# Attention scores in half-row tiles of TensorE, two key chunks at a time, with unpadded keys and a reordered start

## The chip, the cores and the metric

One core of one Trainium2 chip. The metric is the device time of one execution in microseconds (us), taken over several executions on the same chip. A program on one core has no die to compare with, so a run counts as fast when it lies within 1.5% of the fastest of its kernel; all times here are of such runs. Engines: PE is TensorE, ACT is ScalarE, DVE is VectorE, POOL is GpSimd, SP issues transfers. PE's spans are modelled at their ends, so for PE I read starts, not durations.

## The reference

Eight batches of twelve heads, 448 positions, head size 64. Attention with normed queries and keys, then a feed-forward of 768 to 2048 to 768 without residual:

```python
q_n, k_n = (rmsnorm(q, g_q), rmsnorm(k, g_k))
scores = scale * np.matmul(q_n, k_n.transpose(0, 1, 3, 2))
...
attn = attn / (np.sum(attn, axis=-1, keepdims=True) + 1e-09)
return np.matmul(attn, v).astype(np.float32)
...
h = x @ w_in
g = h * (1.0 / (1.0 + np.exp(-1.702 * h)))
return (g @ w_out).astype(np.float32)
```

## The kernel before

Two heads form a head pair; there are 48. Positions are cut into four chunks of 112. The program order of every engine is made ahead of time: `_Order` plays a list of tasks with assumed durations, and emits each instruction when its turn comes there. An engine then runs its instructions strictly in that order. `od.add(name, engine, assumed ns, emit, priority, deps, lat, takes)`; `takes` names a buffer that must be free.

Keys lie zero padded: head 0 in rows 0 to 63 of one block of columns, head 1 in rows 64 to 127 of another, zeros elsewhere, so each score matmul uses all 128 rows of which 64 multiply zeros.

```python
def score(i, kc):                       # head pair i, key chunk kc
    sc = scs[i, kc] = ps_sc.tile([128, 2, 512], FP32, tag="sc", name="sc")   # 2 such buffers
    for hp in range(2):
        nc.tensor.matmul(sc[:SS, hp, :S],
                         lhsT=qk_ring[i % N_KZ][:, NS * (1 + hp) + kc, :],
                         rhs=qk_ring[i % N_KZ][:, :NS, :], start=True, stop=True)

def expo(i, kc):
    nc.scalar.activation(out=att_ring[i % N_ATT][:SS, kc, :, :S],
                         in_=scs.pop((i, kc))[:SS, :, :S], func=ACT.Exp)
...
od.add("gG", "DVE", 350, scale_g, -90, at=5000.0)        # product of the gains, early on DVE
...
od.add(("L", i, w), "SP", 400, ..., lat=moved(830.0))    # a load of 224 KB: 830 ns of the link
od.add(("S", i, j), "ACT", ..., i - 4.5, ...)            # squares for the norms, pair i
...
od.add(("C", i, kc), "PE", 380, lambda i=i, kc=kc: score(i, kc), i + kc / 4, ...,
       takes=("sc", ("E", i, kc)))
od.add(("E", i, kc), "ACT", 917, lambda i=i, kc=kc: expo(i, kc), i + kc / 4 - 1,
       deps=[("C", i, kc), ("P", i - N_ATT, 1, NS - 1)])
```

The value matmuls ("o" in the profile), the first feed-forward matmuls ("gp") and the second ("op") share PE with the scores ("sc"). The feed-forward of a batch can start only when its six head pairs are through attention, so PE has nothing but attention to do at first.

## Time and profile before

| | kernel before |
|---|---|
| time, median | 461.55 us (460.93 to 462.12, 4 runs) |
| span of the profiled execution | 460.4 us |
| first score matmul starts | 16.6 us |
| first feed-forward matmul starts | 55.0 us |
| last matmul ends | 455.6 us |

The two starts cut the run into a first part, in which PE waits for others, and a second, in which PE is the bound. The page's lines are shown in the prediction.

### The profile page before, as it was taken

Reading aid. Unit: us, or ns where it says so; the run is one execution under the profiler, and the core shown is the slowest. Engines: PE = TensorE matmul, PEld = TensorE weight load, DVE = VectorE, ACT = ScalarE, POOL = GpSimd, SP = SyncE. Lnnn points to the kernel's source line nnn. Section 1 sums busy time; section 2 is a strip of 40 time slices with the busy share of each in tenths; the row PEclk is TensorE's granted clock in tenths of the full one; section 3 lists DMA queues with packets and bytes.
Section 4 is the critical chain, followed back from the end, with each engine's and each line's share of the span. In section 5 each row is a group of like instructions: output and inputs, shape, how many; then the busy total and the mean of one; then the engine's idle time right before and its main releaser. Section 6 shows DMA issues by size and latency. Waiting matters only on the chain.

```text
span 460.4 us, 9576 instructions
## 1 busy us (share of the span) xinstructions
PE 435.3 (95%) x3728; PEld 271.9 (59%) x3728; DVE 219.0 (48%) x471; ACT 324.1 (70%) x463; POOL 196.5 (43%) x319
## 2 busy tenths in 40 slices
PE   0589999999999999999999999999999999999995
PEld 0356666666666665666666665666666665665563
DVE  3777888765653446515572347622551125403400
ACT  4587997888887778967886779866786677614421
POOL 4888986975272544434452635445343000000000
PEclk9997999999999999999999999999999999999998
DMA  8999999966868866587675885575323650021022
GB/s 204 266 243 255 250 244 231 214 185 158 163 136 155 234 160 152 130 186 166 155 168 119 216 192 131 124 172 144 66 57 74 105 121 16 17 78 36 0 70 69
DMA packets 111277, 67.48 MB, mean 147 GB/s; under 512 B 70272, under 2 KB 107648, under 8 KB 111232
## 3 DMA queue, kind: packets, MB, share of 16 engines
q1 hardware_dynamic: 105616, 60.35, 56.0%
q0 software_dynamic: 5376, 6.29, 7.8%
q8 instruction: 29, 0.48, 0.5%
q10 hardware_dynamic: 240, 0.23, 0.2%
q14 instruction: 16, 0.13, 0.1%
HBM read 45.61 MB, written 11.01 MB: 123 GB/s over the span
## 4 chain that ended last, share of the span: by engine, by line
PE 88%; POOL 3%; DVE 2%; DMA 2%; ACT 2%; issue 1%; SPq 1%; POOLq 0%; DVEq 0%; ACTq 0%
PE op L514 32%; PE gp L491 30%; PE sc L350 15%; PE o L362 10%; DMA gk<-in_g_k_dram 1%; POOL row L306 1%; ACT att L355 1%; PE t_ps L322 1%; DMA raw<-in_k_dram 1%; PE ot_ps L385 1%; DVE ssq L265 1%; DVE qk L332 0%; DVE obs L373 0%; POOL gq L174 0%; SPq L254 0%
## 5 line engine op out<-in xcount | busy, mean ns | idle before, releaser
L355 ACT ACTIVATE att<-sc 112x896 bf16<-112x896 f32 x192 | 173.9, 916 | 39.9 <-PE sc L350 37.9
L514 PE MATMUL op<-w_out_s,g 128*128 128x384 bf16 x896 | 167.5, 325 | 0.0
L491 PE MATMUL gp<-xt,w_in_s 128*128 128x448 bf16 x768 | 162.6, 352 | 0.0
L306 POOL TENSOR_TENSOR row<-raw,rs 112x512 bf16<-112x512 f32 x96 | 98.3, 1043 | 94.2 <-DMA qk<-row 84.6
L350 PE MATMUL sc<-qk 128*112 128x448 bf16 x384 | 109.4, 370 | 3.0 <-ACT att L355 1.4
L514 PEld LDWEIGHTS <-g 128*128 128x128 bf16 x896 | 81.1, 97 | 47.4 <-issue 0.3
L506 DVE SCALAR_TENSOR_TENSOR g<-th,gp 128x448 bf16<-128x448 f32 x128 | 78.0, 615 | 60.9 <-ACT th L500 60.8
L491 PEld LDWEIGHTS <-w_in_s 128*128 128x128 bf16 x768 | 71.0, 98 | 57.8
L362 PEld LDWEIGHTS <-att 112*128 112x128 bf16 x1536 | 82.2, 99 | 36.8 <-DVE obs L373 1.5
L500 ACT ACTIVATE th<-gp 128x448 f32<-128x448 f32 x128 | 69.3, 543 | 35.3 <-PE gp L491 35.1
L362 PE MATMUL o<-vx,att 112*128 112x65 bf16 x1536 | 90.8, 196 | 0.7 <-ACT att L355 0.4
L313 POOL TENSOR_TENSOR vx<-vraw,ones 112x512 bf16<-112x512 f32 x48 | 50.0, 1042 | 51.6 <-PE o L362 35.8
L265 DVE TENSOR_REDUCE ssq<-sq 112x16 f32<-112x1024 f32 (+1 forms) x50 | 58.4, 1174 | 27.9 <-ACT sq L259 27.7
L372 DVE RECIPROCAL rcp<-o 112x4 f32<-112x4 f32 x96 | 17.4, 181 | 112.0 <-PE o L362 111.4
L259 ACT ACTIVATE sq<-raw 112x1024 f32<-112x1024 f32 (+1 forms) x50 | 50.9, 1022 | 14.3 <-DMA raw<-in_k_dram 9.1
L524 ACT ACTIVATE osb<-op 128x384 f32<-128x384 f32 x56 | 27.3, 487 | 40.4 <-PE op L514 40.4
L350 PEld LDWEIGHTS <-qk 128*112 128x112 bf16 x384 | 44.0, 135 | 17.9 <-issue 4.0
L373 DVE TENSOR_TENSOR obs<-o,rcp 112x256 bf16<-112x256 f32 x96 | 40.7, 424 | 3.3
L343 ACT ACTIVATE qk<-qk,gG 128x448 bf16<-128x448 bf16 x36 | 23.9, 663 | 1.0 <-DMA qk<-row 0.9
L322 PE MATMUL t_ps<-ident,row 112*128 112x112 bf16 x96 | 9.6, 250 | 15.8 <-POOL row L306 15.7
L322 PEld LDWEIGHTS <-row 112*128 112x128 bf16 x96 | 7.2, 117 | 19.0 <-POOL row L306 17.5
L289 POOL TENSOR_TENSOR rs<-magic,seed 112x48 int32<-112x48 int32 (+1 forms) x16 | 4.5, 282 | 20.0 <-DVE seed L280 16.9
(37 smaller groups left out, 90.1 us busy)
## 6 DMA issues: line engine op xcount, KB each, us to landing
raw<-in_q_dram SPq DMA_DIRECT2D x48, 224.0 KB, 4.2
vraw<-in_v_dram SPq DMA_DIRECT2D x48, 224.0 KB, 3.9
raw<-in_k_dram SPq DMA_DIRECT2D x47, 224.0 KB, 4.7
w_in_s<-in_moe_w_in_dram POOLq DMA_DIRECT2D x4, 768.0 KB, 12.8
w_out_s<-in_moe_w_out_dram POOLq DMA_DIRECT2D x4, 768.0 KB, 11.3
out_dram<-osb SPq DMA_DIRECT2D x8, 336.0 KB, 3.3
out_dram<-osb SPq DMA_DIRECT2D x8, 288.0 KB, 2.7
out_dram<-osb SPq DMA_DIRECT2D x8, 240.0 KB, 2.9
```

The source lines that it names most:

```text
L259: nc.scalar.activation(out=sq_of[i][:SS, part], in_=raw[i][:SS, part], func=ACT.Square)
L265: nc.vector.reduce_sum(out=ssq_of[g0][:SS, i - g0, part], in_=sq_of[i][:SS, part], axis=AX.X)
L306: nc.gpsimd.tensor_tensor(out=row_view(i, gi)[:SS], in0=raw[i][:SS, gi], in1=y[:SS, a, gi].to_broadcast([SS, 2, NS, D]), op=ALU.mult)
L313: nc.gpsimd.tensor_tensor(out=vx[:, :, :D], in0=vr, in1=ones[:SS, :].to_broadcast([SS, 2 * NS, D]), op=ALU.mult)
L350: nc.tensor.matmul(sc[:SS, hp, :S], lhsT=qk_ring[i % N_KZ][:, NS * (1 + hp) + kc, :], rhs=qk_ring[i % N_KZ][:, :NS, :], start=True, stop=True)
L355: nc.scalar.activation(out=att_ring[i % N_ATT][:SS, kc, :, :S], in_=scs.pop((i, kc))[:SS, :, :S], func=ACT.Exp)
L362: nc.tensor.matmul(os_[i, hp][:, qs, :], lhsT=att_ring[i % N_ATT][:SS, kc, hp, qs * SS:qs * SS + WIN], rhs=vx_ring[i % N_V][:SS, hp, kc, : ...
L373: nc.vector.tensor_tensor(out=obs[i][:SS, :, hp, :], in0=o[:SS, :, :D], in1=rcp[:SS, :].to_broadcast([SS, NS, D]), op=ALU.mult)
L491: nc.tensor.matmul(ps[:, :], lhsT=w_in_s[:, ki, m * 128:(m + 1) * 128], rhs=xT[b][:, ki, :], start=(ki == 0), stop=(ki == KI - 1))
L500: nc.scalar.activation(out=th[:, :], in_=gps[b, m][:, :], func=ACT.Tanh, scale=0.851)
L506: nc.vector.scalar_tensor_tensor(out=g_of[b // 2][:, m, lo:lo + S], in0=ths.pop((b, m))[:, :], scalar=1.0, in1=gps.pop((b, m))[:, :], op0= ...
L514: nc.tensor.matmul(ops[bp, tm, hf][:, :], lhsT=g_of[bp][:, ko, tm * 128:(tm + 1) * 128], rhs=w_out_s[:, ko, hf * HALF:(hf + 1) * HALF], st ...
```

## The change

Its intent: let both heads' score matmuls run side by side in the two halves of PE's rows, and issue two key chunks together so that PE enters this mode half as often. Padding goes, so the transposing transfer from `row` to `qk` (the "crossbar" of the prediction) turns 8 blocks instead of 12, and DVE places keys with one instruction instead of two. The gains' loads move from POOL's queue to SP's, behind the first five loads, and their product on DVE moves behind the first pair's norms. The assumed durations of some tasks change too. A run of score matmuls with nothing else between them is called a group below; it has two matmuls before and four after.

```diff
-    def score(i, kc):
-        sc = scs[i, kc] = ps_sc.tile([128, 2, 512], FP32, tag="sc", name="sc")
-        for hp in range(2):
-            nc.tensor.matmul(sc[:SS, hp, :S],
-                             lhsT=qk_ring[i % N_KZ][:, NS * (1 + hp) + kc, :],
-                             rhs=qk_ring[i % N_KZ][:, :NS, :], start=True, stop=True)
+    def score(i, kcs):
+        for kc in kcs:
+            sc = scs[i, kc] = ps_sc.tile([128, 2, 512], FP32, tag="sc", name="sc")
+            for hp in range(2):
+                r = slice(64 * hp, 64 * hp + 64)
+                nc.tensor.matmul(sc[:SS, hp, :S], lhsT=qk_ring[i % N_KZ][r, 1, kc, :],
+                                 rhs=qk_ring[i % N_KZ][r, 0], start=True, stop=True)
 ...
-    od.add("gG", "DVE", 350, scale_g, -90, at=5000.0)
+    od.add("Lg", "SP", 1700, load_g, -5.2, lat=3000.0)
+    od.add("gG", "DVE", 350, scale_g, -0.5, deps=["Lg"])
 ...
-        for kc in range(NS):
-            od.add(("C", i, kc), "PE", 380, lambda i=i, kc=kc: score(i, kc), i + kc / 4,
-                   ... takes=("sc", ("E", i, kc)))
+        step = 1 if i < SINGLE else 2          # SINGLE = 2
+        for kc in range(0, NS, step):
+            kcs = range(kc, kc + step)
+            od.add(("C", i, kc), "PE", 190 * step + 130, lambda i=i, kcs=kcs: score(i, kcs),
+                   ... takes=("sc", [("E", i, c) for c in kcs]))
```

More of the change, by code (lines that the diff above doesn't have):

```diff
@@ L84, in run @@
                     if best.takes:
-                        self.slots[best.takes[0]][1].append(best.takes[1])
+                        self.slots[best.takes[0]][1].extend(best.takes[1])
                     best.emit()
@@ L119, in _fits @@
         n, held = self.slots[t.takes[0]]
-        if len(held) < n:
-            return True
-        back = self.named[held[-n]]
-        return back.end is not None and back.end <= now
+        for j in range(len(t.takes[1])):
+            if len(held) + j >= n:
+                back = self.named[held[j - n]]
+                if back.end is None or back.end > now:
+                    return False
+        return True
 @with_exitstack
@@ L153 @@
     ON_PE = NP * 2
+    SINGLE = 2
     ctx.enter_context(tc.manual_schedule())
@@ L170 @@
     gk = consts.tile([128, 1], FP32)
-    for t, src in ((gq, g_q), (gk, g_k)):
-        col = src.rearrange("(d o) -> d o", o=1)
-        for lo in (0, 64):
-            nc.gpsimd.dma_start(out=t[lo:lo + 64, :], in_=col)
     gG = consts.tile([128, 1], FP32)
@@ L180 @@
                 for j in range(N_ATT)]
-    qk_ring = [consts.tile([128, 3 * NS, SS], BF16, name=f"qk{j}", tag=f"qk{j}")
+    qk_ring = [consts.tile([128, 2, NS, SS], BF16, name=f"qk{j}", tag=f"qk{j}")
                for j in range(N_KZ)]
-    row_ring = [consts.tile([128, (3 * NS + 1) * 128], BF16, name=f"row{j}", tag=f"row{j}")
+    row_ring = [consts.tile([128, 2, NS, 128], BF16, name=f"row{j}", tag=f"row{j}")
                 for j in range(N_QKN)]
-    def row_view(j, gi):
-        t = row_ring[j % N_QKN]
-        if gi == 0 or j < ON_PE:
-            t = t[:, gi * NS * 128:(gi + 1) * NS * 128]
-            return t.rearrange("p (n h d) -> p h n d", h=2, d=D)
-        both = t[:, NS * 128:].rearrange("p (h r) -> p h r", h=2)[:, :, :NS * 128]
-        return both.rearrange("p h (n c) -> p h n c", c=128)[:, :, :, :D]
     vx_ring = [consts.tile([128, 2, NS, D + 1], BF16, name=f"vx{j}", tag=f"vx{j}")
                for j in range(N_V)]
-    for t in qk_ring:
-        nc.vector.memset(t[64:128, NS:2 * NS, :], 0.0)
-        nc.vector.memset(t[0:64, 2 * NS:, :], 0.0)
     for t in vx_ring:
@@ L301, in norm @@
         y, a = rs[i]
-        if gi == 1 and ON_PE <= i < ON_PE + N_QKN:
-            c = row_ring[i % N_QKN][:, NS * 128:3 * NS * 128].rearrange("p (n c) -> p n c", c=128)
-            nc.gpsimd.memset(c[:, :NS, D:], 0.0)
-            nc.gpsimd.memset(c[:, NS:, :D], 0.0)
         nc.gpsimd.tensor_tensor(
-            out=row_view(i, gi)[:SS], in0=raw[i][:SS, gi],
+            out=row_ring[i % N_QKN][:SS, gi].rearrange("p n (h d) -> p h n d", h=2), in0=raw[i][:SS, gi],
             in1=y[:SS, a, gi].to_broadcast([SS, 2, NS, D]), op=ALU.mult)
@@ L323, in turn_pe, with take_k @@
                     tps[i][:, gi, s, :],
-                    row_ring[i % N_QKN][:SS, (gi * NS + s) * 128:(gi * NS + s + 1) * 128],
-                    ident[:SS, :SS])
+                    row_ring[i % N_QKN][:SS, gi, s, :], ident[:SS, :SS])
     def take_q(i):
-        nc.vector.tensor_copy(out=qk_ring[i % N_KZ][:, :NS, :], in_=tps[i][:, 0])
-    def take_k(i, hp):
-        r = slice(64 * hp, 64 * hp + 64)
-        nc.vector.tensor_scalar(out=qk_ring[i % N_KZ][r, NS * (1 + hp):NS * (2 + hp), :],
-                                in0=tps[i][r, 1], scalar1=gG[r, :], scalar2=None,
-                                op0=ALU.mult)
+        nc.vector.tensor_copy(out=qk_ring[i % N_KZ][:, 0], in_=tps[i][:, 0])
+    def take_k(i):
+        nc.vector.tensor_scalar(out=qk_ring[i % N_KZ][:, 1], in0=tps[i][:, 1],
+                                scalar1=gG[:, :], scalar2=None, op0=ALU.mult)
     def turn_dma(i):
-        nc.sync.dma_start_transpose(out=qk_ring[i % N_KZ][:, :, :],
-                                    in_=row_ring[i % N_QKN][:SS, :3 * NS * 128])
+        nc.sync.dma_start_transpose(
+            out=qk_ring[i % N_KZ][:, :, :, :].rearrange("p g n s -> p (g n) s"),
+            in_=row_ring[i % N_QKN][:SS].rearrange("s g n c -> s (g n c)"))
     def scale_q(i):
-        t = qk_ring[i % N_KZ][:, :NS, :]
+        t = qk_ring[i % N_KZ][:, 0]
         nc.scalar.activation(out=t, in_=t, func=ACT.Identity, scale=gG[:, :])
     scs, os_ = {}, {}
-    def score(i, kc):
-        sc = scs[i, kc] = ps_sc.tile([128, 2, 512], FP32, tag="sc", name="sc")
-        for hp in range(2):
-            nc.tensor.matmul(sc[:SS, hp, :S],
-                             lhsT=qk_ring[i % N_KZ][:, NS * (1 + hp) + kc, :],
-                             rhs=qk_ring[i % N_KZ][:, :NS, :], start=True, stop=True)
+    def score(i, kcs):
[5 more added lines that the diff above has]
+                                 rhs=qk_ring[i % N_KZ][r, 0], start=True, stop=True)
     def expo(i, kc):
@@ L399, in scale_g, with load_g @@
                                 op0=ALU.mult)
-    od.add("gG", "DVE", 350, scale_g, -90, at=5000.0)
+    def load_g():
+        for t, src in ((gq, g_q), (gk, g_k)):
+            for lo in (0, 64):
+                nc.sync.dma_start(out=t[lo:lo + 64, :], in_=src.rearrange("(d o) -> d o", o=1))
+    od.add("Lg", "SP", 1700, load_g, -5.2, lat=3000.0)
+    od.add("gG", "DVE", 350, scale_g, -0.5, deps=["Lg"])
     for i in range(NG):
@@ L405 @@
         for w in range(3):
-            od.add(("L", i, w), "ACTQ" if i == 0 and w == 1 else "SP", 400,
+            od.add(("L", i, w), "ACTQ" if i == 0 and w == 1 else "SP", 480,
                    lambda i=i, w=w: load(i, w), i - 7 + (0, 0.1, 1.5)[w],
@@ L427 @@
                deps=[("L", i, 2), ("P", i - N_V, 1, NS - 1)])
-        kz_free = [("C", i - N_KZ, NS - 1)]
+        kz_free = [("C", i - N_KZ, NS - 1), ("C", i - N_KZ, NS // 2)]
         if i < ON_PE:
-            od.add(("T", i), "PE", 400, lambda i=i: turn_pe(i), i - 1.0,
-                   deps=[("N", i, 0), ("N", i, 1)], lat=250, takes=("w", ("K", i, 1)))
+            od.add(("T", i), "PE", 420, lambda i=i: turn_pe(i), i - 1.0,
+                   deps=[("N", i, 0), ("N", i, 1)], lat=250, takes=("w", [("K", i)]))
@@ L432 @@
             od.add(("KQ", i), "DVE", 400, lambda i=i: take_q(i), i - 2.0,
                    deps=[("T", i)] + kz_free)
-            for hp in range(2):
-                od.add(("K", i, hp), "DVE", 460, lambda i=i, hp=hp: take_k(i, hp), i - 1.9,
-                       deps=[("T", i), ("KQ", i), ("gG"), ("K", i, hp - 1)] + kz_free)
-        else:
-            od.add(("T", i), "SP", 400, lambda i=i: turn_dma(i), i - 10.0,
-                   deps=[("N", i, 0), ("N", i, 1)] + kz_free, lat=moved(2400.0))
-            od.add(("KQ", i), "ACT", 540, lambda i=i: scale_q(i), i - 1.5,
+            od.add(("K", i), "DVE", 460, lambda i=i: take_k(i), i - 1.9,
+                   deps=[("T", i), ("KQ", i), ("gG")] + kz_free)
+        else:
+            od.add(("T", i), "SP", 1350, lambda i=i: turn_dma(i), i - 10.0,
+                   deps=[("N", i, 0), ("N", i, 1)] + kz_free, lat=moved(1600.0))
+            od.add(("KQ", i), "ACT", 662, lambda i=i: scale_q(i), i - 1.5,
@@ L441 @@
                    deps=[("T", i), ("gG")])
-        for kc in range(NS):
-            od.add(("C", i, kc), "PE", 380, lambda i=i, kc=kc: score(i, kc), i + kc / 4,
-                   deps=[("K", i, 0), ("K", i, 1), ("KQ", i)], lat=250,
-                   takes=("sc", ("E", i, kc)))
-            od.add(("E", i, kc), "ACT", 917, lambda i=i, kc=kc: expo(i, kc), i + kc / 4 - 1,
-                   deps=[("C", i, kc), ("P", i - N_ATT, 1, NS - 1)])
+        step = 1 if i < SINGLE else 2
+        for kc in range(0, NS, step):
+            kcs = range(kc, kc + step)
+            od.add(("C", i, kc), "PE", 190 * step + 130, lambda i=i, kcs=kcs: score(i, kcs),
+                   i + kc / 4, deps=[("K", i), ("KQ", i)], lat=250,
+                   takes=("sc", [("E", i, c) for c in kcs]))
+            for c in kcs:
+                od.add(("E", i, c), "ACT", 917, lambda i=i, c=c: expo(i, c), i + c / 4 - 1,
+                       deps=[("C", i, kc), ("P", i - N_ATT, 1, NS - 1)])
@@ L453 @@
                        + [("P", i, hp, qs - 1)], lat=250,
-                       takes=("o", ("O", i, hp)) if qs == 0 else None)
+                       takes=("o", [("O", i, hp)]) if qs == 0 else None)
             od.add(("O", i, hp), "DVE", 630, lambda i=i, hp=hp: divide(i, hp), i - 2,
@@ L459 @@
             od.add(("B", i), "PE", 200, lambda i=i: back_pe(i), i + 1.5,
-                   deps=[("O", i, 0), ("O", i, 1)], lat=250, takes=("w", ("X", i)))
+                   deps=[("O", i, 0), ("O", i, 1)], lat=250, takes=("w", [("X", i)]))
             od.add(("X", i), "DVE", 390, lambda i=i: take_x(i), i - 1, deps=[("B", i)] + xt_free)
         else:
-            od.add(("X", i), "SP", 400, lambda i=i: back_dma(i), i - 10,
+            od.add(("X", i), "SP", 1220, lambda i=i: back_dma(i), i - 10,
                    deps=[("O", i, 0), ("O", i, 1)] + xt_free, lat=moved(800.0))
@@ L548 @@
                    deps=[("X", b * NP + p) for p in range(NP)] + [("WI", m // 4), last],
-                   lat=250, takes=("w", ("G", b, m)))
+                   lat=250, takes=("w", [("G", b, m)]))
             last = ("F", b, m)
@@ L552 @@
             od.add(("H", b, m), "ACT", 542, lambda b=b, m=m: tanh(b, m), key - 2,
-                   deps=[("F", b, m)], takes=("th", ("G", b, m)))
+                   deps=[("F", b, m)], takes=("th", [("G", b, m)]))
             od.add(("G", b, m), "DVE", 620, lambda b=b, m=m: gate(b, m), key - 2,
@@ L565 @@
                            + [("WO", c), last], lat=250,
-                           takes=("w", ("U", bp, tm, hf)) if c == 0 else None)
+                           takes=("w", [("U", bp, tm, hf)]) if c == 0 else None)
                     last = ("Y", bp, tm, hf, c)
@@ L570 @@
                        lambda bp=bp, tm=tm, hf=hf: take_out(bp, tm, hf), key - 2,
-                       deps=[last], takes=("osb", ("D", bp, tm)) if hf == 0 else None)
+                       deps=[last], takes=("osb", [("D", bp, tm)]) if hf == 0 else None)
             od.add(("D", bp, tm), "SP", 1200, lambda bp=bp, tm=tm: store(bp, tm), key + 1,
```

## The prediction

> **What bounds the kernel now.** I read the page's busy shares first, then its slices, to see whether the busiest engine is busy everywhere:
>
> ```profile
> PE 435.3 (95%) x3728; PEld 271.9 (59%) x3728; DVE 219.0 (48%) x471; ACT 324.1 (70%) x463; POOL 196.5 (43%) x319
> PE   0589999999999999999999999999999999999995
> ACT  4587997888887778967886779866786677614421
> PE 88%; POOL 3%; DVE 2%; DMA 2%; ACT 2%; issue 1%; SPq 1%; POOLq 0%; DVEq 0%; ACTq 0%
> ```
>
> TensorE (PE) is at nine tenths or more from the fourth slice (about 35 us) to the last but one, and is 88% of the chain that ended last. Busy time is not work, as matmuls overlap, so I asked what PE waited for. From 60 to 398 us, nearly all of the attention, the waits of all engines name PE as the one waited for, and in 60 to 120 us PE itself waits once:
>
> ```profile
> PE sc L350 <- ACT att L355: 0.3, 1, 0.3
> ```
>
> So between about 56 us and the end at 456 us an ns saved on PE is an ns saved on the run. In the first 56 us the chain passes through every engine; there PE is not the bound. The price of each kind of matmul comes from start-to-start times in PE's timeline, not from its mean duration:
>
> ```profile
> 244.22 0.81 PE L514 MATMUL op<-w_out_s,g 128*128 128x384 bf16 x4
> 244.88 0.54 PE L350 MATMUL sc<-qk 128*112 128x448 bf16 x2
> 245.25 0.29 PE L362 MATMUL o<-vx,att 112*128 112x65 bf16 x4
> 245.39 0.49 PE L514 MATMUL op<-w_out_s,g 128*128 128x384 bf16 x2
> ```
>
> The two score matmuls hold PE from 244.88 to 245.25, 0.37 us; eight such places near 240 to 256 us give 0.37 to 0.40, so I take 0.385. There are 384 score matmuls, 192 pairs: 192 x 0.385 = 73.9 us, a sixth of the run. Changing between score, value (o) and feed-forward (op) matmuls costs nothing visible now: 0.81 us for four op matmuls lasts until 245.03, but the next starts at 244.88.
>
> **What the Trainium skill says.** "TensorE: Matmul & The Clock Gate", section "Single matmul latency", gives (398 + N)/2.4 ns warm. For N = 448 that is 352.5; the trace's median score matmul is 353, so it agrees. The same page, "Part 3: Packing small matmuls", says that matmuls in different row groups run side by side, started about 4 ns apart, and that four tiles of 32 rows gained 3.07 times; no matmul in this trace uses half the rows, so nothing here shows it. "TensorEngine Tiling (Array Packing)", section "Key Properties", says that a change of tiling mode drains TensorE, without a figure; this trace has no mode change. Its "Gotcha 1: PSUM Pressure" forbids two row tiles in one PSUM bank at once; the two heads go to separate 512-column halves of sc, so I expect no collision.
>
> **The change part by part.**
>
> 1. Scores. Before, each head's keys fill 64 of the 128 rows and zeros fill the rest, so two heads cost two full passes. After, head 0 uses rows 0 to 63 and head 1 rows 64 to 127: two matmuls should share one pass. To size a pass: op takes 326 ns for 384 columns and o 194 ns for 65, so a column costs (326 - 194)/(384 - 65) = 0.414 ns and the fixed part is 194 - 27 = 167 ns. A pass of 448 columns is 185 ns; four matmuls, now 770 ns, become two passes, 371 ns.
>
> 2. The entry fee. Score weights (112 columns) load in 130 ns, the 128-column ones in 98; I estimate that 112 columns at 0.414, 46 ns, are really occupied. After a drain the first load cannot hide: +46 ns.
>
> 3. The mode changes: one in, one out. If emptying the array cost the whole fixed part, each would be 167 ns; if nothing, 0. [...]I choose two fifths, 67 ns each, 134 for both. This is a choice between limits, not a reading, and it is the weakest term. Group of four: 371 + 46 + 134 = 551 ns against 770, so 0.219 us saved. The instruction order built from the changed kernel has 95 unbroken runs of scores (94 of four, one of eight), against 180 before, with nothing of another mode inside a run. 95 x 0.219 = 20.8 us, all on PE, from which the start's few groups are too few to subtract.
>
> 4. Pair wise issue. Both sc buffers must be free before a group starts, and ScalarE (ACT) then waits for new scores. One group of 0.55 us plus two exponentials of 0.917 and some 0.3 of hand-offs is 2.7 us, 5.4 per head pair, while a pair takes about (398 - 17)/48 = 7.9 us now and some 7.5 after. In the gap ACT has squares, tanh and copies to do: its load from 60 to 398 us is 264 of 338 us, 78%, and would be 83%. I add nothing.
>
> 5. Keys by VectorE, for the first 12 head pairs: one instruction over 128 rows instead of two over 64 (0.46 each). 12 x 0.46 = 5.5 us of DVE, which is 48% busy; on the chain only a few times before 56 us.
>
> 6. Crossbar turns: 36 of 8 blocks instead of 12. They now land after 3.6 us; a third less data may cut that to about 3. GpSimd (POOL) waits 84.6 us for them, but POOL is not on the chain after 56 us: worth nothing there.
>
> 7. The start. The gains g_q, g_k came by GpSimd's queue; the chain reads:
>
> ```profile
> 3.22 6.28 DMA gk<-in_g_k_dram
> 9.62 0.57 DVE gG L397
> 12.54 2.33 DVE ssq L265 x3
> ```
>
> DVE stood 3.0 us for them before it could form the first pair's inverse norms. In the new order this product comes after those norms, so the first pair starts up to 3 + 0.7 us sooner. But pairs 1 and 2 need raw keys that landed at 10.4 us, and the four small loads now sit in front of them in the sync engine's queue: 4 x 0.46 us of issue. I count 1.5 us, by judgement. The memsets of qk and row on DVE and POOL ran in idle time: 0.
>
> Sum: 20.8 + 1.5 = 22.3; 462.1 - 22.3 = 439.8, say 440 us.
>
> **Rivals.**
>
> a. The drains eat the gain. With 167 ns each way and both weight loads bare, a group is 371 + 46 + 334 + about 13 = 764 ns: no gain, about 460 us. For it: the skill says drain, and the new order enters and leaves the mode 95 times. Against: doing two key chunks per entry halves the number of entries.
>
> b. The two halves do not run side by side. Then four passes, 740 ns, plus drains: 0.1 to 0.3 us worse per group, 470 to 490 us. For it: only that this trace has no such matmul. Against: the skill's 3.07 for four tiles.
>
> c. ACT becomes the bound: its 324 us is below 440, but taking sc buffers in twos could leave PE waiting for exponentials when the static order is off. In the trace ACT waits 37.9 us for scores and PE 1.4 us for ACT; it has room. If a quarter of the 95 groups waited 0.4 us, that is 10 us: about 450.
>
> d. The end binds. After the last score group PE still has 224 op, 108 gp and 40 o matmuls by the new order; from the last stretch (128 op in 20.8, 96 gp in 18.2 us) that is 36 + 20 + 1 = 58 us, as now. The saving lies before it and is not lost.
>
> **Range and chances.** With drains free, group = 417, saving 33.5 + 1.5: 427. With full drains: about 460. I centre on 440 and give 428 to 457 for 8 in 10. Faster by over 2% needs under 452.8, that is 82 ns or more per group with the start's 1.5: 0.77. Within 2%: 0.16. Slower needs rival b or bad waits: 0.07.
>
> **What would show it.** PE's timeline should show four score matmuls followed by the next kind 0.45 to 0.65 us later, and two score matmuls starting within some tens of ns. A spacing of 0.75 or more proves a or b: gaps at the run's edges mean a, even starts 0.19 us apart inside mean b. More than 5 us of PE waiting on ACT att means c. The first score should start at 13 to 16 us, not 16.6. The time is wrong most probably through the 67 ns per mode change: each 50 ns there, both ways, moves it by 9.5 us.

## The result, and the profile after

The changed kernel takes 455.6 us (455.46 to 456.74, 4 runs), 0.988 of the time before with a 95% interval of 0.985 to 0.990. A ratio here is the mean time of one kernel's fast runs over that of the other's fast runs of the same rounds, so not quite the ratio of the medians. The gain is real and about 6 us, where 22 were forecast; it is under 2%. The time lies just inside the range.

The page of the kernel after, first the busy shares, then the slices and the chain:

```profile
PE 423.0 (93%) x3728; PEld 244.4 (54%) x3728; DVE 211.9 (47%) x453; ACT 319.2 (70%) x463; POOL 193.2 (42%) x309
...
PE   0676799999999999999999999999999999999995
...
ACT  4665798887887878877887878976786667514411
...
PE 86%; DMA 8%; DVE 2%; ACT 2%; SPq 1%; issue 0%; ACTq 0%; DVEq 0%
```

From the second slice on, PE's row began 5, 8, 9, 9 and now begins 6, 7, 6, 7, and transfers hold 8% of the chain instead of 2%: the first part of the run is worse. The second part is better. PE's timeline there (start, us, engine, line, operation, count):

```profile
240.14 0.42 PE L345 MATMUL o<-vx,att 112*128 112x65 bf16 x8
240.49 0.59 PE L334 MATMUL sc<-qk 64*112 64x448 bf16 x4
241.01 0.82 PE L505 MATMUL op<-w_out_s,g 128*128 128x384 bf16 x4
```

Four score matmuls stand from 240.49 to 241.01, 0.52 us, where two pairs took 0.77. But eight value matmuls now keep PE from 240.14 to 240.49, 0.35 us; at the 32.7 ns apiece of the kernel before, they would take 0.26. The group's fee is partly paid by its neighbour.

From the start times of single matmuls (medians of 69 groups between 100 and 380 us) a group reads:

| step in a group of four | ns | without mode change |
|---|---|---|
| last matmul before it (of 65, 384, 448 columns) to the first score | 124, 255, 282 | 33, 162, 189 |
| first head to second head, both passes | 3 | 190 |
| second head to the next pass's first | 230 | 189 |
| last score to the next kind of matmul | 282 | 189 |
| first to second matmul of the next kind | 39, 173, 199 | 34, 162, 189 |

So the group takes 3 + 230 + 3 + 282 = 518 ns, and its neighbours pay 93 before and some 10 after: 621 ns against 770. Two passes of 189 ns are in it; the other 243 ns are the price of the entry.

Start to start summed by kind from the first feed-forward to the last score matmul, and the rest of the run:

| | before | after |
|---|---|---|
| first score matmul | 16.6 us | 13.7 us |
| first feed-forward matmul | 55.0 us | 59.7 us |
| ns for each sc / o / gp / op from there to the last score | 196.9 / 32.7 / 189.2 / 162.5 | 129.1 / 37.1 / 193.0 / 165.1 |
| last matmul ends | 455.6 us | 449.7 us |

The second part shrank from 400.7 to 390.0 us, by 10.7; the first grew by 4.8; together 5.9 us less. In the first part, here is ACT before (its timeline; idle time and who ended it in brackets):

```profile
35.59 1.06 ACT L259 ACTIVATE sq<-raw 112x1024 f32<-112x1024 f32 x1 [1.14 <-DMA raw<-in_k_dram]
...
40.34 6.23 ACT L355 ACTIVATE att<-sc 112x896 bf16<-112x896 f32 x7 [0.20 <-PE sc L350]
```

(`att<-sc` are the exponentials, `sq<-raw` the squares for the norms, `raw` the queries and keys as loaded)

and after:

```profile
35.83 1.06 ACT L246 ACTIVATE sq<-raw 112x1024 f32<-112x1024 f32 x1 [5.24 <-DMA raw<-in_k_dram]
39.60 1.06 ACT L246 ACTIVATE sq<-raw 112x1024 f32<-112x1024 f32 x1 [2.71 <-DMA raw<-in_k_dram]
40.56 3.33 ACT L338 ACTIVATE att<-sc 112x896 bf16<-112x896 f32 x4
45.00 1.72 ACT L338 ACTIVATE att<-sc 112x896 bf16<-112x896 f32 x2 [1.10 <-PE sc L334]
48.28 1.72 ACT L338 ACTIVATE att<-sc 112x896 bf16<-112x896 f32 x2 [1.55 <-PE sc L334]
```

ACT's waits from 14 to 60 us (who waited for whom: us, times, longest), the first line before, the others after:

```profile
ACT att L355 <- PE sc L350: 7.2, 8, 2.9
...
ACT sq L246 <- DMA raw<-in_k_dram: 12.3, 5, 5.2
ACT att L338 <- PE sc L334: 4.1, 5, 1.6
```

Two things are to be seen. ACT stands 5.24 and 2.71 us in front of squares whose raw keys have not landed, while exponentials that could run come later in its fixed order. And where seven exponentials ran back to back, they now come two by two with gaps of over 1 us; in total, though, ACT waits less for scores than before (4.1 against 7.2 us), as raw keys hold it up first. A third is seen in the clock: the page's row starts 9, 9, 6, 5, 7, 8 (before: 9, 9, 9, 7, 9, 9), and value matmuls stand 49 to 55 ns apart from 16 to 48 us, where before they stood 32 to 35 apart from 28 us on but for 36 to 40. I call this the half clock, as feed-forward matmuls in such a stretch stand 370 ns apart instead of 189 (e9, below). The clock row alone does not always show it: in e1 it is 9 throughout, with value matmuls 50 to 55 ns apart from 16 to 60 us. Which of these three cost the start is what the experiments are for.

### The profile page after: what moved, and what is told of

Same layout as the page of the kernel before. It is cut to its first block, busy times and chain, and to the rows that moved or that the text cites. A ratio compares the mean times of both kernels' runs of the same rounds, so it can differ in the third digit from the quotient of the medians.

```text
span 455.0 us, 9525 instructions
## 1 busy us (share of the span) xinstructions
PE 423.0 (93%) x3728; PEld 244.4 (54%) x3728; DVE 211.9 (47%) x453; ACT 319.2 (70%) x463; POOL 193.2 (42%) x309
## 4 chain that ended last, share of the span: by engine, by line
PE 86%; DMA 8%; DVE 2%; ACT 2%; SPq 1%; issue 0%; ACTq 0%; DVEq 0%
PE op L505 32%; PE gp L482 32%; PE o L345 12%; PE sc L334 10%; DMA raw<-in_k_dram 5%; DMA raw<-in_q_dram 2%; DMA gq<-in_g_q_dram 1%; ACT att L338 1%; DVE obs L356 1%; DVE ssq L252 0%; SPq L241 0%; PE ot_ps L368 0%; PE t_ps L305 0%; DVE g L497 0%; DVE rcp L355 0%
## 5 line engine op out<-in xcount | busy, mean ns | idle before, releaser
L338 ACT ACTIVATE att<-sc 112x896 bf16<-112x896 f32 x192 | 167.3, 914 | 22.3 <-PE sc L334 21.1
L505 PE MATMUL op<-w_out_s,g 128*128 128x384 bf16 x896 | 162.8, 326 | 0.0
L482 PE MATMUL gp<-xt,w_in_s 128*128 128x448 bf16 x768 | 160.5, 353 | 0.2
L345 PEld LDWEIGHTS <-att 112*128 112x128 bf16 x1536 | 79.2, 101 | 55.3 <-issue 23.3
L497 DVE SCALAR_TENSOR_TENSOR g<-th,gp 128x448 bf16<-128x448 f32 x128 | 78.5, 618 | 60.6 <-ACT th L491 60.4
L505 PEld LDWEIGHTS <-g 128*128 128x128 bf16 x896 | 79.7, 97 | 48.4 <-issue 4.4
L345 PE MATMUL o<-vx,att 112*128 112x65 bf16 x1536 | 95.2, 200 | 5.4 <-DVE obs L356 2.9
L482 PEld LDWEIGHTS <-w_in_s 128*128 128x128 bf16 x768 | 68.9, 98 | 57.9 <-issue 4.2
L252 DVE TENSOR_REDUCE ssq<-sq 112x16 f32<-112x1024 f32 (+1 forms) x50 | 58.6, 1174 | 38.9 <-ACT sq L246 36.7
L334 PE MATMUL sc<-qk 64*112 64x448 bf16 x384 | 61.3, 394 | 5.7 <-ACT att L338 4.3
L334 PEld LDWEIGHTS <-qk 64*112 64x112 bf16 x384 | 18.9, 131 | 22.8 <-issue 17.2
```

The lines of the kernel that those rows point to most:

```text
L252: nc.vector.reduce_sum(out=ssq_of[g0][:SS, i - g0, part], in_=sq_of[i][:SS, part], axis=AX.X)
L334: nc.tensor.matmul(sc[:SS, hp, :S], lhsT=qk_ring[i % N_KZ][r, 1, kc, :], rhs=qk_ring[i % N_KZ][r, 0], start=True, stop=True)
L345: nc.tensor.matmul(os_[i, hp][:, qs, :], lhsT=att_ring[i % N_ATT][:SS, kc, hp, qs * SS:qs * SS + WIN], rhs=vx_ring[i % N_V][:SS, hp, kc, : ...
L482: nc.tensor.matmul(ps[:, :], lhsT=w_in_s[:, ki, m * 128:(m + 1) * 128], rhs=xT[b][:, ki, :], start=(ki == 0), stop=(ki == KI - 1))
L497: nc.vector.scalar_tensor_tensor(out=g_of[b // 2][:, m, lo:lo + S], in0=ths.pop((b, m))[:, :], scalar=1.0, in1=gps.pop((b, m))[:, :], op0= ...
L505: nc.tensor.matmul(ops[bp, tm, hf][:, :], lhsT=g_of[bp][:, ko, tm * 128:(tm + 1) * 128], rhs=w_out_s[:, ko, hf * HALF:(hf + 1) * HALF], st ...
```

## The experiments

Fifteen kernels ran (no run has the label e3), all correct, each timed against the kernel before on the same chip. "First gp" is the start of the first feed-forward matmul in the profiled execution, so it comes from one execution each. Theories A to C are set out in the expectation of e1, E and F in that of e6, G in that of e10; there is no D. Executions of one kernel differ here more than those of the kernel before: e1 took 454.0 to 459.7 us, e6 451.3 to 456.4, e9 454.5 to 459.3, the kernel before 460.5 to 463.7 over all rounds. Medians that differ by 1 or 2 us are therefore not told apart.

| run | what differs (from the changed kernel, if not said otherwise) | median us | ratio to before | first gp us |
|---|---|---|---|---|
| changed kernel | | 455.6 | 0.988 | 59.7 |
| e1 | gains loaded by POOL again | 457.0 | 0.989 | 62.1 |
| e2 | weights asked for 3 us later | 456.8 | 0.988 | 60.4 |
| e4 | before + gains' move alone | 463.4 | 1.003 | 57.5 |
| e5 | one chunk at a time throughout | 471.5 | 1.020 | 56.0 |
| e6 | loads reckoned at 1000 ns | 455.3 | 0.985 | 59.2 |
| e7 | early scores computed twice | 458.9 | 0.993 | 61.0 |
| e8 | whole start undone | 458.0 | 0.993 | 59.2 |
| e9 | one chunk in the first 9 pairs | 458.2 | 0.991 | 60.6 |
| e10 | e6 and e9 together | 450.0 | 0.973 | 54.2 |
| e11 | filler matmuls | 456.4 | 0.987 | 56.9 |
| e12 | e10 and filler | 451.5 | 0.977 | 55.8 |
| e13 | before + two chunks at a time | 468.6 | 1.014 | 61.2 |
| e14 | e12 without the last fillers | 450.7 | 0.976 | 54.8 |
| e15 | e11 without the last fillers | 457.6 | 0.991 | 56.2 |
| e16 | e10 with the old start | 452.2 | 0.979 | 57.4 |

**Is it the gains' loads? (e1)** In these traces SP never has more than eight transfers in flight; in the trace after, the four tiny loads take such places from 2.7 to 9 us.

```diff
+    for t, src in ((gq, g_q), (gk, g_k)):
+        ... nc.gpsimd.dma_start(out=t[lo:lo + 64, :], in_=col)
-    od.add("Lg", "SP", 1700, load_g, -5.2, lat=3000.0)
-    od.add("gG", "DVE", 350, scale_g, -0.5, deps=["Lg"])
+    od.add("gG", "DVE", 350, scale_g, -0.5, at=9000.0)
```

> The changed kernel with one part undone: g_q and g_k are loaded by GpSimd's queue at the start again (their product on VectorE stays late, after the first pair's norms). Theory A, the four tiny loads take places among the few transfers that the sync queue has in flight, so the raw loads of pairs 2 and on start 2.5 us later and the start is lost through that: raw keys of pair 8 land at 31 us or sooner (35.7 in the changed kernel), first feed-forward matmul at 54 to 56 us instead of 59.7, run 450 to 452 us instead of 455.6. Theory B, the loss comes from the weights' transfers that start 3 us sooner: nothing is gained, 455 to 457 us, first feed-forward matmul still 59 to 60. Theory C, issue by pairs of chunks costs it: the same as B.

457.0 us, first gp at 62.1, raw keys of pair 8 at 36.6: nothing is won, so theory A falls. The first loads were issued as early as in the kernel before, yet by 20 us they landed 1 to 1.5 us behind its times again.

**Do the weights' transfers crowd them out? (e2)**

```diff
-        od.add(("WI", c), "POOL", 900, ..., -50, at=13000.0 + 6500.0 * c,
+        od.add(("WI", c), "POOL", 900, ..., -50, at=16000.0 + 6500.0 * c,
```

> The changed kernel with the first weights' transfers asked for 3 us later in the order's own reckoning; nothing else. Theory B (the weights take bandwidth from the raw loads in the first 40 us): raw keys of pair 8 land before 33 us, first feed-forward matmul by 57 us, run 451 to 453 us. Theories A and C: no gain, 455 to 457 us.

The raw keys of pair 8 did come sooner, at 32.9 instead of 35.7 us, as theory B has it, but the first gp stayed at 60.4 and the time at 456.8. The transfers do crowd each other; mending that alone buys nothing.

**The gains' move alone (e4)**

```diff
 (on the kernel before)
-            nc.gpsimd.dma_start(out=t[lo:lo + 64, :], in_=col)
-    od.add("gG", "DVE", 350, scale_g, -90, at=5000.0)
+    od.add("Lg", "SP", 1700, load_g, -5.2, lat=3000.0)
+    od.add("gG", "DVE", 350, scale_g, -0.5, deps=["Lg"])
```

> The kernel before with only the start of the change: g_q and g_k on the sync queue after the first five loads and their product late. Scores stay zero padded, one chunk at a time. Theory A: the start is lost here too, in spite of the earlier norms: first feed-forward matmul at 58 to 60 us instead of 55.0, run 464 to 467 us against 461.6. Theory C (the loss belongs to the pairs of chunks): the start gains 1 to 3 us, 459 to 461 us.

The first score came at 13.7 us and the first gp at 57.5, 2.5 us later than before; 463.4 us, 1.003 of before (0.0 to 0.5% longer). Less than theory A asked, the opposite of theory C's gain: an earlier first score did not carry through.

**One chunk at a time throughout (e5)**

```diff
-        step = 1 if i < SINGLE else 2
+        step = 1
```

> The changed kernel with one key chunk at a time throughout: 192 entries into the half-row mode instead of 96. From the changed kernel's trace one group of two should cost 3 + 282 ns to the next matmul's start, 93 ns on the matmul before it and some 8 after: 386 ns, just what a zero padded pair costs (385). So packing without pairing should gain nothing on TensorE: from the first feed-forward matmul on, 164 groups of 386 against 82 of 613 ns is 13 us more than in the changed kernel, run 467 to 470 us if the start stays as it is, 463 to 466 if the single chunks also mend the start (theory C). If the mode changes cost less when they are more frequent, under 460 us.

471.5 us, slower than before, and slower than I forecast. The start went back to 56.0 us, although ACT still waited 10.4 us for raw keys. But in the second part a group of two took 329 ns, not 285, with 93 ns before it and 11 after: 433 ns against 385 for a padded pair. That is one pass of 189 and 244 ns besides, as many as the 243 of a group of four: the fee goes by the entry, and the second pass costs just its 189. Packing pays only because two chunks share one entry. So pairing is needed where PE is the bound, and the start says that it hurts where PE is not.

**ACT's order (e6)**

```diff
-                   lat=moved(830.0))        # of the raw loads
+                   lat=moved(1000.0))
```

> The changed kernel with one number of the order's reckoning altered: a raw load takes 1000 ns of the link instead of 830 (the chip moved 215 to 231 GB/s in the first 20 us, so 224 KB take about 1000 ns). ScalarE's fixed order then holds the squares of pairs 8 and 9 behind exponentials of pairs 3 and 4. Theory E, the lost start is ScalarE standing in front of a square whose raw keys have not landed while scores wait: its waits for raw keys from 14 to 60 us fall from 12.3 to under 4 us, first feed-forward matmul at 53 to 56 us, run 449 to 452 us. Theory F, the half clock alone: waits fall but the score groups stay at 0.92 us and the first feed-forward matmul at 58 to 60, run 454 to 457 us.

ACT's waits for raw keys fell from 12.3 to 3.5 us, as theory E wanted, and pair 3's exponentials were done at 38.1 instead of 43.9 us. Yet the first gp came at 59.2 and the time is 455.3: the next pairs took 5.6, 6.2 and 7.5 us each, and the lead was gone. Theory E alone falls.

**The half clock, first try (e7)**

```diff
+        for _ in range(2 if 2 <= i < 9 else 1):
             for kc in kcs:
                 ... (the same matmuls again)
```

> The changed kernel with each score group of pairs 2 to 8 computed twice over (same operands, same result), so that TensorE has more to do from 20 to 60 us; nothing else moves in any engine's order. Theory F, TensorE is too idle there, its clock halves, and matmuls of 1.06 and 0.92 us where 0.53 and 0.52 were due lengthen the path: with more work the groups of value matmuls return to 0.53 us before 50 us, first feed-forward matmul at 56 to 58 us, run 452 to 454 us in spite of the added work. Theory E (waits of ScalarE for raw keys): no gain, 456 to 460 us.

458.9 us: worse, and value matmuls still stood 53 to 55 ns apart up to 48 us. The doubled work lies on the path, so this run decides nothing; e14 and e15 ask better.

**The whole start undone (e8)**

```diff
+            nc.gpsimd.dma_start(out=t[lo:lo + 64, :], in_=col)     # as before
+    od.add("gG", "DVE", 350, scale_g, -90, at=5000.0)              # as before
```

> The changed kernel with its whole new start undone: gains by GpSimd's queue, their product first on VectorE as before, so the first score returns to 16.6 us. If the earlier start itself makes transfers collide (weights at 15.8 us), the start is as before: raw keys of pair 8 at 31 us, first feed-forward matmul at 55 us, run 450 to 452 us. If pairing is what breaks the start, it stays at 58 us or later, run 454 to 458 us.

First score at 16.2 us, raw keys of pair 8 at 31.6 (30.4 before), and still first gp at 59.2 and 458.0 us. With the old start and nearly the old landings, the start is lost all the same: that leaves pairing, or the half clock (value matmuls 54 to 55 ns apart from 20 to 40 us).

**One chunk in the first nine pairs (e9)**

```diff
-    SINGLE = 2
+    SINGLE = 9
```

> The changed kernel with one key chunk at a time in the first 9 head pairs instead of the first 2, before TensorE is the bound. If pairing breaks the start, the first feed-forward matmul comes at 55 to 56 us (as with single chunks throughout, 56.0) and the run takes 451 to 453 us; if ScalarE's waits for raw keys do, little changes: 58 to 60 us, run 455 to 457 us.

458.2 us (454.5 to 459.3), first gp at 60.6. ACT waited 9.0 us for raw keys. So these four executions gained nothing. But e5, with single chunks and the same load time, had its first gp at 56.0, and up to there the two are the same program: the first 430 matmuls come in the same order in both (to 63.6 us in e5), and so do ACT's first 54 instructions. Up to 47 us they also run within about half a us of each other, and from 41 us on ACT waits for no transfer in either. Then they part; PE in e5, then in e9:

```profile
47.65 0.40 PE L334 MATMUL sc<-qk 64*112 64x448 bf16 x2
48.80 0.69 PE L345 MATMUL o<-vx,att 112*128 112x65 bf16 x16
55.95 1.31 PE L482 MATMUL gp<-xt,w_in_s 128*128 128x448 bf16 x6
57.10 0.42 PE L345 MATMUL o<-vx,att 112*128 112x65 bf16 x8
```

```profile
48.05 0.62 PE L334 MATMUL sc<-qk 64*112 64x448 bf16 x2
50.02 1.06 PE L345 MATMUL o<-vx,att 112*128 112x65 bf16 x16
60.62 2.42 PE L482 MATMUL gp<-xt,w_in_s 128*128 128x448 bf16 x6
62.84 0.65 PE L345 MATMUL o<-vx,att 112*128 112x65 bf16 x8
```

The six feed-forward matmuls stand 192 ns apart in e5 and 370 in e9; the granted clock from 20 to 60 us was 0.87 and 0.62. In e5 the full clock was back at 48 us, in e9 not before 63, and e9's first gp came 4.7 us later. So e9 does not show that unpairing buys nothing: its profiled execution lost to the half clock what e5's gained.

**Both (e10)** puts e6 and e9 together.

> The changed kernel with two causes taken away at once: one key chunk at a time in the first 9 head pairs, and loads reckoned at 1000 ns so that ScalarE's order does not stand in front of late raw keys. Theory G, the start is lost to several things that each take turns (late raw keys, TensorE and ScalarE in lockstep when both score buffers go together, the half clock): both together bring the first feed-forward matmul to 52 to 56 us and the run to 448 to 452 us. If the half clock alone decides, it stays at 58 to 60 us and 454 to 457.

450.0 us (447.6 to 450.8), 0.973 of before, first gp at 54.2. Either mend alone gave 455.3 and 458.2; both give 450.0, and no execution of e10 was as slow as the fastest of e6 (451.3) or e9 (454.5). The causes hide each other. ACT's waits in e10 from 14 to 60 us:

```profile
ACT sq L246 <- DMA raw<-in_k_dram: 7.0, 2, 4.2
ACT att L338 <- PE sc L334: 4.1, 7, 1.4
```

The clock was at half here too for most of the time up to 48 us. The waits for raw keys are not gone (7.0 us), but they no longer stand in front of pair 3: its exponentials were done at 39.0 us, and pairs 4, 5 and 6 followed 4.4, 5.2 and 4.5 us apart, where the changed kernel took 6.1, 5.1 and 5.7 after 43.9.

**Pairing alone, on the kernel before (e13)** keeps padded keys and the old start.

```diff
 (on the kernel before)
-        for kc in range(NS):
-            od.add(("C", i, kc), "PE", 380, lambda ...: score(i, kc), ..., takes=("sc", ("E", i, kc)))
+        step = 1 if i < 2 else 2
+        for kc in range(0, NS, step):
+            od.add(("C", i, kc), "PE", 380 * step, lambda ...: score(i, kcs), ...,
+                   takes=("sc", [("E", i, c) for c in kcs]))
```

> The kernel before, zero padded keys and its own start, with scores issued two chunks at a time from the third head pair on, as the change does. The four matmuls of a group take 0.77 us as two pairs did. If taking both score buffers at once costs nothing, 461 to 462 us; lockstep in the first 60 us should cost it 2 to 5 us: first feed-forward matmul at 57 to 60 us, run 463 to 467 us, with ScalarE waiting more on scores than the 7.2 us from 14 to 60 us of the kernel before.

468.6 us, 1.014 of before, first gp at 61.2: pairing alone moves the start by 6.2 us, more than forecast. The waits of ACT, then its timeline:

```profile
ACT att L361 <- PE sc L356: 11.6, 9, 2.9
...
ACT sq L264 <- DMA raw<-in_k_dram: 0.2, 1, 0.2
```

```profile
39.92 1.72 ACT L361 ACTIVATE att<-sc 112x896 bf16<-112x896 f32 x2 [1.28 <-PE sc L356]
42.47 1.72 ACT L361 ACTIVATE att<-sc 112x896 bf16<-112x896 f32 x2 [0.82 <-PE sc L356]
46.61 1.72 ACT L361 ACTIVATE att<-sc 112x896 bf16<-112x896 f32 x2 [2.42 <-PE sc L356]
```

and PE in the same stretch:

```profile
44.76 1.03 PE L368 MATMUL o<-vx,att 112*128 112x65 bf16 x16 [1.70 <-DVE obs L379]
45.60 1.72 PE L356 MATMUL sc<-qk 128*112 128x448 bf16 x4
```

Raw keys play no part here (0.2 us), and value matmuls stood 32 to 33 ns apart from 28 to 44 us (53 in the line above), so the clock plays little. What is seen is lockstep: a group may start only when both score buffers are free, that is when ACT is through with the exponentials of both; and PE's fixed order has sixteen value matmuls ahead of it, which wait 1.70 us for DVE to free their one buffer. ACT waits 2.42 us. With single chunks one buffer can be full while the other is refilled. How much of the 6.2 us is the wait for both buffers, and how much the coarser order that puts sixteen value matmuls in front, no run separates. After the first gp nothing was lost: from there to the last matmul e13 took 399.9 us, the kernel before 400.7.

**Filler (e11 on the changed kernel, e12 on e10; then e15 and e14)** adds matmuls on constants, never read, where the order reckons PE idle:

```diff
+    def filler():
+        ps = ps_w.tile([128, S], FP32, tag="w", name="fl")
+        for _ in range(2):
+            nc.tensor.matmul(ps[:, :], lhsT=ident[:, :], rhs=fill[:, :], start=True, stop=True)
+    for j in range(60):
+        od.add(("Z", j), "PE", 380, filler, 1000 + j, at=12000.0 + 500.0 * j,
+               takes=("w", [("Z", j)]))
```

> The changed kernel with filler: pairs of full matmuls on constants, never read, in places where the order reckons TensorE idle from 12 us on; nothing is added to the work that others wait for. Theory F (half clock): score groups and value groups return to full speed before 40 us (0.52 and 0.53 us instead of 0.92 and 1.06), first feed-forward matmul at 55 to 57 us, run 451 to 453 us. If late raw keys and lockstep decide alone, the clock comes back but the run stays at 455 to 458 us.

> All three together: single chunks for 9 pairs, loads at 1000 ns, filler. Theory G: first feed-forward matmul at 50 to 54 us, run 445 to 450 us, the best of all. If it is no better than the one without filler, the half clock does not matter.

The clock came back: value matmuls 32 to 33 ns apart from 20 to 60 us in both. The times are 456.4 and 451.5 us. 20 and 26 filler matmuls (10 and 13 pairs) ended up at the very end and kept PE busy there for 4 to 5 us, but after the last feed-forward matmul, while the last results were still on their way out: from that matmul's end to the end of the span 5.2 us passed in e11 and 5.9 in e12, against 5.3 in the changed kernel and 5.0 in e10. So at most 0.9 us is theirs. Both ran again with 49 and 46 fillers instead of 60:

> The changed kernel with only the 49 fillers placed before 60 us (the earlier run had 10 more at the end and took 456.4). If the half clock is part of the lost start, 451 to 454 us against 455.6; first feed-forward matmul near 57 us as before. If not, 455 to 457.

> The mended kernel (single chunks for 9 pairs, loads at 1000 ns, 450.0 us) with only the 46 fillers that the order places before 60 us; the earlier filler run had 13 more after the last score group and took 451.5. If the half clock costs something on the path, 445 to 448 us; if it lies wholly in idle time, 449 to 451 us.

457.6 us for the changed kernel with filler, 450.7 us for the mended one, against 455.6 and 450.0 without. Full clock, no gain in the time: the half clock alone is not the lost start, and theory F by itself falls. It is not without weight, though. In e15 the first gp was 3.5 us sooner; but pair 7's exponentials were done at 68.6 us, as in the changed kernel (68.5), so the lead was given back within 13 us. There ACT stood 2.42 us for the raw keys of a square that began at 58.9, DVE 3.9 us in front of the sum behind it, and PE 2.1 us for the value buffer that DVE frees after that sum. Filler on e9, which would ask whether single chunks and the full clock are enough without the truer load time, did not run.

**The earlier start under the mended kernel (e16)** is e10 with the gains handled as before.

> The mended kernel with the old start (gains by GpSimd, their product first on VectorE, first score at 16.2 instead of 13.7 us). If the earlier start is worth what it gains at the first score, this is 2 to 3 us slower than 450.0: 452 to 453 us. If transfers bind the first 55 us, it makes no difference: 449 to 451 us.

452.2 us, 2.2 more than e10 (95% intervals of the ratio 0.9763 to 0.9813 and 0.9705 to 0.9757), with the first score 3.3 us later and the first gp 3.2 later. Once the other two limits are mended, the earlier start is worth what it seemed to be.

## Why the prediction was wrong, point by point

**The bound.** Right for the second part: from 60 us to its end, PE waited for another engine once, 0.8 us. The reading behind it was too wide: the waits from 60 to 398 us do not all name PE (POOL waited 84.6 us for transfers, DVE 38.9 for ACT); what holds is that PE itself did not wait.

**Step 1, side by side.** Right: 3 ns between the two heads' starts. Rival b is refuted. The pass was sized at 185 ns from durations, whose ends are modelled; from start to start it is 189.

**Steps 2 and 3, the fees.** The mechanism was right, the size was not, and it was the term named as weakest. "67 ns each" for the mode changes measured 93 each: leaving, 282 less 189 ns; entering, 93 before the first score. In all 69 groups the first weights begin to load 2 ns before the first score matmul, where in the kernel before they began a median of 187 ns before theirs, so their "+46" is not in the 93. It answers to the 41 between the two passes: the second pass's weights are no cause of that, as they begin to load 47 ns after the first pass starts and are in 60 ns before the second one; and with one pass (e5) as much turns up on leaving, 326 ns instead of 282. That the 41 are the first load is my reading; that they go with the entry and not with the second pass is shown. Not in the sum at all: some 10 after the group. The passes themselves are 13 longer than I had them. That makes 26 + 26 - 5 + 10 + 13 = 70: 621 ns instead of 551; saved 149 ns per group instead of 219. Over the 82 groups after the first gp that is 82 x 0.070 = 5.7 us less. Rival a, 764 ns, was 143 off on the other side.

**The count.** I let all 95 runs of scores save time and called the start's "too few to subtract". Thirteen lie before the first gp, where PE is not the bound: 13 x 0.219 = 2.8 us that did not exist. Counted rightly, 82 x 0.149 = 12.2 us, and that is what the second part's costs per matmul add up to (scores 22.2 less; o 5.7, gp 2.5 and op 1.7 more; 12.3 net). The span of the second part fell by 10.7, as 16 value and 4 score matmuls more now lie in it, some 1.3 us at the old prices.

**Step 4, "I add nothing".** This is the step that failed outright. I checked whether ACT had time in the steady state, where PE has other work, and it does. I did not check the first 56 us, where the chain "passes through every engine" by my own words, and where both score buffers at once stop ACT and PE by turns. e13 measures it without the rest of the change: first gp 6.2 us later and 1.4% more time. In the changed kernel late raw keys and the half clock join it, and no run tells the three shares apart. Rival c named the wait and asked for more than 5 us of PE waiting on ACT; from 14 to 60 us the trace shows 4.3 us before scores and 1.7 before value matmuls, 6.0 in all. I gave it as a quarter of all groups, where it is the start alone.

**Step 7, the start "1.5 us".** The first score did come 2.9 us sooner, and the first gp 4.8 us later. The step stopped at the first score. On the kernel before (e4) the sooner start made the first gp 2.5 us later; under the mended kernel (e10, e16) it is worth 2.2 us of the run.

**Steps 5 and 6.** Their zero in the second part can stand: no wait of PE there leads to them. No run undid them alone, nor the other assumed durations that changed.

**The sum.** Forecast 22.3 us, counted from the profiled execution's 462.1 (the median is 461.55). Less 5.7 for the fees, 2.8 for the count, and for the start 1.5 + 4.8 + 1.3 = 7.6: 6.2 remain, and the profiled spans show 5.9 at PE's last matmul. With the fees and the count as measured and the start as forecast, 13.8 us (3%) would have been left: it is the start, steps 4 and 7, that took the change below 2%. My range had room for this at its upper end, but 0.77 for "faster by over 2%" trusted the start that I had not worked out.

What stays open: how much of the lost start belongs to each of pairing, late raw keys and the half clock. e6 and e9 gained nothing alone, and each one's profile names what took over (pairs 5.6 to 7.5 us apart in e6; the half clock up to 63 us and 9.0 us of raw keys in e9). e5 against e9 shows that the clock moves the first gp by 4.7 us with the same order of work, so a first gp read from one execution is no firm measure; why the full clock was back at 48 us in e5 and not before 63 in e9 no run shows. Why the raw keys of pair 8 land later when scores start sooner is only partly shown: weights asked for later bring them forward (e2), and with the old start they land at 31.1 to 31.6 us (e8, e13, e16).

## What to carry to other kernels

A packing mode of PE has to be priced with its entry, its exit and its neighbours: here four matmuls saved 252 ns by themselves and 149 after the fees, and two matmuls at a time lost time. Taking all buffers of a ring at once was free where PE had other work (e13: 399.9 against 400.7 us in the second part) and cost 6.2 us where it had none, so make the batch small until the pipeline is full (e10: 450.0 us, the lowest median of all, is the changed kernel with single chunks for nine pairs and a truer load time). When several causes sit in series, undoing one alone can show nothing; try them together before dropping any. And before a mend is called useless, compare its profile with a run that has the same order up to there: e5 and e9 had, and the clock made 4.7 us between them.

## What the Trainium skill lacked or had wrong

- "TensorEngine Tiling (Array Packing)", "Key Properties", says that a mode change drains TensorE, but gives no figure: here 93 ns to enter, 93 to leave, 41 to 44 that go with the first pass and about 10 on the first matmul after, 243 to 244 ns for an entry whether it holds one pass or two. With two matmuls to an entry the packed form took 433 ns against 385 padded, which the page's table "Theoretical Speedup" (up to 2 times for a dimension of 64 or less) does not lead one to expect; with four it took 621 against 770.
- "TensorE: Matmul & The Clock Gate", Part 3, "What overlaps and what doesn't", says that weight loads overlap running matmuls only when the row group differs (the same Part, under "The mechanism", also allows it for a load into a background weight buffer). Taken alone that sentence is too narrow. In full-row mode the padded score matmuls followed each other at 189 to 190 ns, the pace of feed-forward matmuls with as many columns, with a weight load of 130 ns for each, so the load overlapped. In half-row mode the second pass's weights, on the same rows, began to load 47 ns after the first pass had started and were in 60 ns before the second one.
- No page I used prices the taking of all buffers at once: 6.2 us of the start in e13.
